# Taking a fused attention and gated MLP batch by batch instead of in pairs, with q loaded in long runs and turned by VectorE

## The chip, the cores and the metric

The kernel runs on one core of a Trainium2 chip. The metric is the device time of one execution in microseconds. Each timed kernel ran on the same chip as the kernel before; the rounds of both are compared. A kernel counts as faster or slower only from 2% on.

## The reference

Eight batches, eight heads, 576 tokens, 64 channels a head; all in float32, but the three MLP weights come as float64. Cut to what matters:

```python
kv  = einsum('bhsd,bhse->bhde', k, v)
out = einsum('bhsd,bhde->bhse', q, kv)           # no softmax: a 64x64 matrix per head
x   = out / sqrt(mean(out*out, -1) + 1e-6) * g_norm   # then [batch, token, head*channel]
gate_pre = sum of 5 taps of a causal convolution along the tokens, per channel
result   = (sigmoid(gate_pre) * (x @ w_val)) @ w_out
```

## The kernel before

Batches go in pairs: 2 x 576 tokens are nine chunks of 128 tokens. Per chunk, TensorE (PE) turns q, ScalarE copies it out of PSUM, PE multiplies it with kv (`raw`; kv itself is summed by PE and copied by DVE to `kvbd`, a tile with two heads' kv on its diagonal), ScalarE squares, VectorE (DVE) sums, GpSimd takes the root, DVE scales (`x`), PE turns x and ScalarE copies it out (`xT`). Then the MLP of the pair: `gate` (one copy and four taps, then a sigmoid), `val`, `gv = val * gate`, `out`. The program lists a pair's attention beside the MLP of the pair before it. A scheduler in the builder then fixes the order of the instructions on each engine.

```python
def unit_turn_q(i, c):                       # pair i, chunk c
    pq = ps("tp", [P, HP, P], ...)
    for hp in range(HP):
        nc.tensor.transpose(pq[:, hp, :], st["q", i, c][:, 2 * hp:2 * hp + 2, :], ident[:])
    qT = work.tile([P, HP, P], FP32, tag="qT", bufs=3, ...)
    nc.scalar.copy(out=qT[:], in_=pq[:])
    ...
def unit_gate(i, jt):                        # 1152 tokens at a time
    ...
    for tap in range(K - 2, -1, -1):
        back = K - 1 - tap
        nc.vector.scalar_tensor_tensor(out=gb[:, :, back:S], in0=xb[:, :, 0:S - back], ...)
    nc.scalar.activation(out=gate[:], in_=gate[:], func=AF.Sigmoid)
def unit_out(i, c):
    po = ps("mm", [P, C], ...)               # val and out share three PSUM buffers
    ...
    ot = work.tile([P, C], FP32, tag="ot", bufs=3, ...)
    nc.scalar.copy(out=ot[:], in_=po[:])
    nc.scalar.dma_start(out=rows_out[row:row + P, :], in_=ot[:])      # ScalarE's queue
...
for i in range(NP + 1):
    before = mlp(i - 1) if i > 0 else [... conversions of the weights ...]
    merge(attention(i) if i < NP else [], before)
```

Of the kernel before, what the change touches and what calls it, by code (L numbers as in the profile page):

```python
# [9 lines left out]
FP32 = mybir.dt.float32  # L10
U32 = mybir.dt.uint32
AF = mybir.ActivationFunctionType
# [8 lines left out]
def kernel(  # L21
# [11 lines left out]
    """Batches go in pairs: 2 * 576 tokens are nine full chunks of 128, the middle one half of each.  # L33

    The attention's output is normalised in [token, channel], where a head's channels lie in a row,
    and then goes to [channel, token], in which the convolution is a sum of shifted rows and the
    two products need no further transpose.

    The three MLP weights come as float64, in raw bits: the chip rounds them to float32, the widest
    type that its engines compute in.  # L40
    """
    nc = tc.nc
    B, H, S, D = q.shape
    C = H * D                # channels
    HP = H // 2              # pairs of heads: 128 channels each
    NJ = S // P              # full chunks of a batch
    SF = NJ * P
    T = S - SF               # tokens of a batch behind them
    NK = C // P
    NP = B // 2  # L50
    S2 = 2 * S               # tokens of a pair
    NC = S2 // P             # chunks of a pair
    NV = 3                   # parts of a pair's tokens in the value product
    SV = S2 // NV
    K = moe_conv_w.shape[0]
    assert 2 * T == P and NC * P == S2 and SV <= 512 and C <= 512
# [10 lines left out]
    # k's and v's last T tokens; the rows behind them stay zero.  # L67
# [6 lines left out]
    # Both heads' kv on the diagonal, zeros beside them.  # L74
    kv_bd = []
    for i in range(4):
        t = const.tile([P, HP, P], FP32, name=f"kvbd{i}")
        nc.vector.memset(t[:], 0.0)
        kv_bd.append(t)
# [4 lines left out]

    st = {}

    def load_kv(b):
        for n, (name, src) in enumerate((("k", k), ("v", v))):
            st[name, b] = []
            for i in range(2):  # L90
                t = loads.tile([P, H // 2, NJ, D], FP32, tag=f"{name}{i}", name=f"{name}{i}_{b}")
                nc.sync.dma_start(
                    out=t[:].rearrange("p h j d -> p h (j d)"),
                    in_=src[b, i * H // 2:(i + 1) * H // 2, 0:SF, :].rearrange(
                        "h (p j) d -> p h (j d)", j=NJ),
                )
                st[name, b].append(t)
            nc.sync.dma_start(
                out=tails[b % 2][n][0:T], in_=src[b, :, SF:S, :].rearrange("h s d -> s h d"),
            )  # L100

    def batches(i, c):
        """A chunk's rows of each batch: (rows, batch, first token)."""
        lo, hi = c * P, (c + 1) * P
        found = []
        for bb in range(2):
            first, end = max(lo, bb * S), min(hi, (bb + 1) * S)
            if first < end:
                found.append((slice(first - lo, end - lo), 2 * i + bb, first - bb * S))
        return found  # L110

    def load_q(i, c):
        t = loads.tile([P, H, D], FP32, tag="q", bufs=NC, name=f"q{i}_{c}")
        for rows, b, first in batches(i, c):
            nc.sync.dma_start(
                out=t[rows],
                in_=q[b, :, first:first + rows.stop - rows.start, :].rearrange("h s d -> s h d"),
            )
        st["q", i, c] = t

    load_kv(0)
    for c in range(NC):
        load_q(0, c)
        if c == 1:
            load_kv(1)
# [14 lines left out]
    def narrow(key, dst):  # L140
        """In words of a value's bits: lo has the mantissa's lower 32, hi its upper 20 below the
        exponent and the sign. Beyond float32's exponents it gives zero and infinity."""
# [5 lines left out]
        # The exponent in float32's bias, kept within 0..255, in its place, with the sign.  # L148
# [13 lines left out]
        # The mantissa times 2**20: a whole number, with lo behind its point.  # L162
# [20 lines left out]
    # The norm is a sum here, not a mean: its root of D goes to the gain.  # L183
# [14 lines left out]
    def unit_kv(b, hp):  # L198
# [4 lines left out]
        for j in range(NJ + 1):  # L203
            for r in range(2):
                half, h = divmod(2 * hp + r, H // 2)
                nc.tensor.matmul(  # L206
                    kvp[r * D:(r + 1) * D, hp, :],
                    st["k", b][half][:, h, j, :] if j < NJ else kl[:, 2 * hp + r, :],
                    st["v", b][half][:, h, j, :] if j < NJ else vl[:, 2 * hp + r, :],
                    start=(j == 0), stop=(j == NJ),  # L210
                )
        if hp == HP - 1:
            for r in range(2):
                rows = slice(r * D, (r + 1) * D)
                nc.vector.tensor_copy(kv_bd[b % 4][rows, :, rows], kvp[rows])
            if b + 2 < B:
                load_kv(b + 2)

    def unit_turn_q(i, c):
        pq = ps("tp", [P, HP, P], f"qTps{i}_{c}")  # L220
        for hp in range(HP):
            nc.tensor.transpose(pq[:, hp, :], st["q", i, c][:, 2 * hp:2 * hp + 2, :], ident[:])  # L222
        qT = work.tile([P, HP, P], FP32, tag="qT", bufs=3, name=f"qT{i}_{c}")
        nc.scalar.copy(out=qT[:], in_=pq[:])  # L224
        st["qT", i, c] = qT
        if i + 1 < NP:
            load_q(i + 1, c)

    def unit_norm(i, c):
        qT = st["qT", i, c]  # L230
        raw = ps("raw", [P, C], f"raw{i}_{c}")
        for hp in range(HP):
            for rows, b, _ in batches(i, c):
                nc.tensor.matmul(  # L234
                    raw[rows, hp * P:(hp + 1) * P], qT[:, hp, rows],
                    kv_bd[b % 4][:, hp, :],
                    start=True, stop=True,
                )
        sq = work.tile([P, C], FP32, tag="sq", name=f"sq{i}_{c}")
        nc.scalar.activation(out=sq[:], in_=raw[:], func=AF.Square)  # L240
        ss = work.tile([P, H], FP32, tag="ss", bufs=3, name=f"ss{i}_{c}")
        nc.vector.reduce_sum(  # L242
            out=ss[:], in_=sq[:].rearrange("p (h e) -> p h e", h=H), axis=AX.X,
        )
        nc.gpsimd.tensor_scalar(  # L245
            out=ss[:], in0=ss[:], scalar1=D * EPS, scalar2=None, op0=ALU.add,
        )
        rt = work.tile([P, H], FP32, tag="rt", bufs=3, name=f"rt{i}_{c}")
        nc.gpsimd.tensor_tensor(out=rt[:], in0=ss[:], in1=mhalf[:], op=ALU.pow)  # L249
        x = work.tile([P, C], FP32, tag="x", bufs=4, name=f"x{i}_{c}")  # L250
        nc.vector.tensor_tensor(  # L251
            out=x[:].rearrange("p (h e) -> p h e", h=H),
            in0=raw[:].rearrange("p (h e) -> p h e", h=H),
            in1=rt[:].unsqueeze(2).broadcast_to((P, H, D)),
            op=ALU.mult,
        )
        st["x", i, c] = x

    def unit_turn_x(i, c):
        if c == 0:  # L260
            st["xT", i] = work.tile([P, NK, S2], FP32, tag="xT", name=f"xT{i}")
        px = ps("tp", [P, NK, P], f"xTps{i}_{c}")
        for kc in range(NK):
            nc.tensor.transpose(px[:, kc, :], st["x", i, c][:, kc * P:(kc + 1) * P], ident[:])  # L264
        nc.scalar.activation(  # L265
            out=st["xT", i][:, :, c * P:(c + 1) * P], in_=px[:], func=AF.Copy, scale=gcol[:],
        )

    def unit_gate(i, jt):
        x = st["xT", i][:, jt, :]  # L270
        gate = work.tile([P, S2], FP32, tag="gate", bufs=3, name=f"gate{i}_{jt}")
        nc.scalar.activation(out=gate[:], in_=x, func=AF.Copy, scale=cwT[:, jt, K - 1:K])  # L272
        xb = x.rearrange("p (b s) -> p b s", b=2)
        gb = gate[:].rearrange("p (b s) -> p b s", b=2)
        for tap in range(K - 2, -1, -1):
            back = K - 1 - tap
            nc.vector.scalar_tensor_tensor(  # L277
                out=gb[:, :, back:S], in0=xb[:, :, 0:S - back], scalar=cwT[:, jt, tap:tap + 1],
                in1=gb[:, :, back:S], op0=ALU.mult, op1=ALU.add,
            )  # L280
        nc.scalar.activation(out=gate[:], in_=gate[:], func=AF.Sigmoid)  # L281
        st["gate", i, jt] = gate

    def unit_val(i, jt):
        gv = work.tile([P, S2], FP32, tag=f"gv{jt}", bufs=1, name=f"gv{i}_{jt}")
        for n in range(NV):
            cols = slice(n * SV, (n + 1) * SV)
            val = ps("mm", [P, SV], f"val{i}_{jt}_{n}")
            for kc in range(NK):
                nc.tensor.matmul(  # L290
                    val[:], wval[:, kc, jt * P:(jt + 1) * P], st["xT", i][:, kc, cols],
                    start=(kc == 0), stop=(kc == NK - 1),
                )
            nc.vector.tensor_tensor(  # L294
                out=gv[:, cols], in0=val[:], in1=st["gate", i, jt][:, cols], op=ALU.mult,
# [90 lines left out]
```

## Time and profile before

| | before |
|---|---|
| median, rounds of the changed kernel | 407.05 us (406.83 to 407.52, 4 runs) |
| span of the profiled run | 406.9 us |
| PE busy | 358.3 us, 88% |
| first val to the next pair's first val | 86.6 us for two batches, 43.3 a batch |

A pair in the middle of the trace, from val to val (the columns are the stretch, its length and the busy time of PE, its weight loads, DVE, ScalarE and GpSimd, with the number of records; then granted clock, DMA share and GB/s; a record is one instruction of the trace, and a float32 product shows as two: val's 192 products are the 384 records of L290 on its page):

```profile
160.00:246.57 86.57, 85.33 (x485) 52.41 (x481) 41.01 (x50) 29.58 (x45) 19.32 (x18) 1.00 0.43 110
```

The waits of PE in the trace before, besides those for the first loads (columns: who waited, for whom, us in total, times, longest):

```profile
PE val L290 <- DVE gv L294: 12.9, 4, 5.6
PE raw L234 <- DVE x L251: 9.4, 2, 6.7
PE xTps L264 <- DVE x L251: 3.9, 2, 2.1
```

Eight waits that matter, all but two of them (1.0 us each) at the start and at the last pair. The row of TensorE's granted clock in 40 slices (9 is full):

```profile
PEclk9989698769999999999999999999999999799999
```

Behind the start it is full, but for one slice near the end, behind PE's wait for the last pair's gates.

### The profile page before, as it was taken

Reading aid. Unit: us, or ns where it says so; the run is one execution under the profiler, and the core shown is the slowest. Engines: PE = TensorE matmul, PEld = TensorE weight load, DVE = VectorE, ACT = ScalarE, POOL = GpSimd, SP = SyncE. Lnnn points to the kernel's source line nnn. Section 1 sums busy time; section 2 is a strip of 40 time slices with the busy share of each in tenths; the row PEclk is TensorE's granted clock in tenths of the full one; section 3 lists DMA queues with packets and bytes.
Section 4 is the critical chain, followed back from the end, with each engine's and each line's share of the span. In section 5 each row is a group of like instructions: output and inputs, shape, how many; then the busy total and the mean of one; then the engine's idle time right before and its main releaser. Section 6 shows DMA issues by size and latency. Waiting matters only on the chain.

```text
span 406.9 us, 4827 instructions
## 1 busy us (share of the span) xinstructions
PE 358.3 (88%) x1924; PEld 221.1 (54%) x1924; DVE 197.3 (48%) x274; ACT 122.1 (30%) x178; POOL 82.1 (20%) x87
## 2 busy tenths in 40 slices
PE   0665776769999999999999999899999994999996
PEld 0554654536665555656655555666655552555442
DVE  6368666987432212995431126986222129951000
ACT  1023432443122335333133334422223352120111
POOL 2042644002323211005131130024232110000000
PEclk9989698769999999999999999999999999799999
DMA  7999999491272231293713310000011210000222
GB/s 231 301 275 252 288 278 187 129 208 52 66 170 77 79 103 53 84 239 117 156 52 103 93 64 26 2 2 0 2 52 52 76 54 0 0 2 1 77 77 77
DMA packets 69398, 42.28 MB, mean 104 GB/s; under 512 B 47355, under 2 KB 63739, under 8 KB 69376
## 3 DMA queue, kind: packets, MB, share of 16 engines
q1 hardware_dynamic: 62848, 28.32, 30.5%
q10 hardware_dynamic: 5344, 9.44, 6.6%
q0 software_dynamic: 1184, 4.22, 3.1%
q8 instruction: 15, 0.25, 0.3%
q14 instruction: 7, 0.06, 0.1%
HBM read 32.53 MB, written 9.44 MB: 103 GB/s over the span
## 4 chain that ended last, share of the span: by engine, by line
PE 78%; DVE 10%; POOL 3%; ACT 3%; DMA 3%; issue 1%; SPq 1%; POOLq 0%; ACTq 0%
PE out L304 31%; PE val L290 29%; PE raw L234 8%; DVE gate L277 5%; PE kv L206 4%; PE xTps L264 3%; DMA vl<-in_v_dram 3%; PE qTps L222 3%; POOL rt L249 2%; DVE ss L242 1%; DVE x L251 1%; ACT gate L281 1%; POOL ss L245 1%; ACT gate L272 1%; DVE gv L294 1%
## 5 line engine op out<-in xcount | busy, mean ns | idle before, releaser
L290 PE MATMUL val<-xT,wval 128*128 128x384 f32 x384 | 134.7, 507 | 13.0 <-DVE gv L294 12.9
L304 PE MATMUL out<-wout,gv 128*128 128x512 f32 x288 | 128.5, 593 | 0.0
L290 PEld LDWEIGHTS val<-xT,wval 128*128 128x128 f32 x384 | 74.2, 198 | 63.6 <-DVE gv L294 14.2
L277 DVE SCALAR_TENSOR_TENSOR gate<-xT,cwT,gate 128x1148 f32<-128x1148 f32 (+3 forms) x64 | 86.8, 1407 | 18.4 <-ACT gate L272 18.2
L304 PEld LDWEIGHTS out<-wout,gv 128*128 128x128 f32 x288 | 52.6, 190 | 56.3 <-issue 56.0
L249 POOL TENSOR_TENSOR rt<-ss,mhalf 128x8 f32<-128x8 f32 x36 | 60.1, 1668 | 3.0
L245 POOL TENSOR_SCALAR ss<-ss 128x8 f32<-128x8 f32 x36 | 16.2, 449 | 215.0 <-DVE ss L242 214.8
L251 DVE TENSOR_TENSOR x<-raw,rt 128x512 f32<-128x512 f32 x36 | 24.9, 692 | 70.6 <-POOL rt L249 62.9
L309 ACT COPY ot<-out 128x512 f32<-128x512 f32 x36 | 21.1, 586 | 110.0 <-PE out L304 110.0
L242 DVE TENSOR_REDUCE ss<-sq 128x8 f32<-128x512 f32 x36 | 24.6, 682 | 53.5 <-ACT sq L240 53.5
L234 PE MATMUL raw<-kvbd,qT 128*128 128x128 f32 (+1 forms) x320 | 41.5, 289 | 9.4 <-DVE x L251 9.4
L234 PEld LDWEIGHTS raw<-kvbd,qT 128*128 128x128 f32 (+1 forms) x320 | 36.8, 185 | 17.5 <-issue 12.1
L240 ACT ACTIVATE sq<-raw 128x512 f32<-128x512 f32 x36 | 21.5, 598 | 56.3 <-PE raw L234 56.2
L206 PE MATMUL kv<-v,k 128*64 128x64 f32 x512 | 25.7, 250 | 14.3 <-DMA v<-in_v_dram 14.3
L224 ACT COPY qT<-qTps 128x512 f32<-128x512 f32 x36 | 20.8, 587 | 51.9 <-PE qTps L222 51.7
L294 DVE TENSOR_TENSOR gv<-val,gate 128x384 f32<-128x384 f32 x48 | 25.4, 553 | 22.4 <-PE val L290 20.4
L206 PEld LDWEIGHTS kv<-v,k 128*64 128x64 f32 x512 | 21.9, 160 | 22.3 <-issue 21.9
L281 ACT ACTIVATE gate<-gate 128x1152 f32<-128x1152 f32 x16 | 18.6, 1167 | 50.3 <-DVE gate L277 50.3
L265 ACT ACTIVATE xT<-xTps,gcol 128x512 f32<-128x512 f32 x36 | 24.4, 689 | 8.1 <-PE xTps L264 8.1
L264 PE MATMUL xTps<-ident,x 128*128 128x128 f32 x144 | 22.1, 282 | 3.9 <-DVE x L251 3.9
L264 PEld LDWEIGHTS xTps<-ident,x 128*128 128x128 f32 x144 | 17.7, 145 | 12.8 <-issue 12.8
L222 PE MATMUL qTps<-ident,q 128*128 128x128 f32 x144 | 22.8, 292 | 0.7 <-ACT qT L224 0.7
(45 smaller groups left out, 111.6 us busy)
## 6 DMA issues: line engine op xcount, KB each, us to landing
out_dram<-ot ACTq DMA_DIRECT2D x36, 256.0 KB, 2.0
k<-in_k_dram SPq DMA_DIRECT2D x16, 512.0 KB, 5.1
v<-in_v_dram SPq DMA_DIRECT2D x16, 512.0 KB, 7.8
q<-in_q_dram SPq DMA_DIRECT2D x32, 256.0 KB, 6.5
w_wval<-in_moe_w_val_dram POOLq DMA_DIRECT2D x4, 512.0 KB, 7.6
w_wout<-in_moe_w_out_dram POOLq DMA_DIRECT2D x4, 512.0 KB, 7.0
kl<-in_k_dram SPq DMA_DIRECT2D x8, 128.0 KB, 5.8
vl<-in_v_dram SPq DMA_DIRECT2D x8, 128.0 KB, 8.3
```

The lines of the kernel that those rows point to most:

```text
L206: nc.tensor.matmul(kvp[r * D:(r + 1) * D, hp, :], st["k", b][half][:, h, j, :] if j < NJ else kl[:, 2 * hp + r, :], st["v", b][half][:, h, ...
L222: nc.tensor.transpose(pq[:, hp, :], st["q", i, c][:, 2 * hp:2 * hp + 2, :], ident[:])
L234: nc.tensor.matmul(raw[rows, hp * P:(hp + 1) * P], qT[:, hp, rows], kv_bd[b % 4][:, hp, :], start=True, stop=True,)
L242: nc.vector.reduce_sum(out=ss[:], in_=sq[:].rearrange("p (h e) -> p h e", h=H), axis=AX.X,)
L249: nc.gpsimd.tensor_tensor(out=rt[:], in0=ss[:], in1=mhalf[:], op=ALU.pow)
L251: nc.vector.tensor_tensor(out=x[:].rearrange("p (h e) -> p h e", h=H), in0=raw[:].rearrange("p (h e) -> p h e", h=H), in1=rt[:].unsqueeze( ...
L264: nc.tensor.transpose(px[:, kc, :], st["x", i, c][:, kc * P:(kc + 1) * P], ident[:])
L265: nc.scalar.activation(out=st["xT", i][:, :, c * P:(c + 1) * P], in_=px[:], func=AF.Copy, scale=gcol[:],)
L277: nc.vector.scalar_tensor_tensor(out=gb[:, :, back:S], in0=xb[:, :, 0:S - back], scalar=cwT[:, jt, tap:tap + 1], in1=gb[:, :, back:S], op0 ...
L290: nc.tensor.matmul(val[:], wval[:, kc, jt * P:(jt + 1) * P], st["xT", i][:, kc, cols], start=(kc == 0), stop=(kc == NK - 1),)
L294: nc.vector.tensor_tensor(out=gv[:, cols], in0=val[:], in1=st["gate", i, jt][:, cols], op=ALU.mult,)
L304: nc.tensor.matmul(po[:], st["gv", i, jt][:, c * P:(c + 1) * P], wout[:, jt, :], start=(jt == 0), stop=(jt == NK - 1),)
```

## The change

Its intent: no transposes of q on PE and no copies of them on ScalarE, and q's transfers in runs of some 4 kB instead of 256 B. For that q is loaded twice, so that a DVE transpose in 32 x 32 blocks puts it into [channel, token]. The blocks give the token order (n, t), in which token t*18+n stands at n*32+t; a shift of the convolution by one token is then a shift by 32 columns, with four halo rows before each batch in x. Batches go one by one. An output chunk holds four values of n, so it goes out in four transfers, and these are put on the queue of the loads. Batch 1's k and v are loaded last, behind the q of batches 0 and 1. The core of the diff:

```diff
+    def load_q(b, hp):
+        ...
+        for half in range(2):
+            for r in range(2):
+                nc.sync.dma_start(out=flat[first:first + TB, 0:run],
+                    in_=q[b, 2 * hp + r].rearrange("(t n) d -> t (n d)", t=TB)[...])
...
-    def unit_turn_q(i, c):
-        pq = ps("tp", [P, HP, P], f"qTps{i}_{c}")
-        for hp in range(HP):
-            nc.tensor.transpose(pq[:, hp, :], st["q", i, c][:, 2 * hp:2 * hp + 2, :], ident[:])
-        qT = work.tile([P, HP, P], FP32, tag="qT", bufs=3, name=f"qT{i}_{c}")
-        nc.scalar.copy(out=qT[:], in_=pq[:])
+    def unit_turn_q(b, hp):
+        ...
+        nc.vector.transpose(out=st["qT", b][:, hp, :], in_=st["q", b, hp][:, :, 0:TB])
...
+            for kc in range(NK):             # halo rows, on GpSimd
+                row = xT[:, kc, :].rearrange("p (n t) -> p n t", t=TB)
+                nc.gpsimd.tensor_copy(row[:, 0:K - 1, 1:TB], row[:, NB:NB + K - 1, 0:TB - 1])
...
-        gate = work.tile([P, S2], FP32, tag="gate", bufs=3, name=f"gate{i}_{jt}")
+        gate = work.tile([P, S], FP32, tag="gate", bufs=4, name=f"gate{b}_{jt}")
...
-        nc.scalar.dma_start(out=rows_out[row:row + P, :], in_=ot[:])
+        for j in range(HB):
+            bb, n = divmod(c * HB + j, NB)
+            nc.sync.dma_start(
+                out=rows_out[2 * i + bb, n], in_=ot[j * TB:(j + 1) * TB, :])
...
-    for i in range(NP + 1):
+    for b in range(B + 1):
```

## The prediction

Some passages of the prediction are cut, each cut marked. Terms of its sums go with them, those for DVE's turn of q. With these terms in, DVE's work came to about 240 us, the conversions, turns and kvbd of the start to 29 us, and the first gv to 7 us behind its stage's first val; what is still printed adds up to less. The forecast's last sum has all its terms in print, 120 + 293 + 39 = 452, said as 450; in the 120 and the 293 the turns are counted. That an engine keeps to its listed order was taken as given; in this case e13 and e14 show it, further down (their records follow the given lists one for one).

> **What bounds the kernel now.** I read the page's shares first, then the chain of work that ended last, then the order of time on TensorE (PE) in the middle, because a share over the whole span mixes a slow start with a dense middle.
>
> ```profile
> PE 358.3 (88%) x1924; PEld 221.1 (54%) x1924; DVE 197.3 (48%) x274; ACT 122.1 (30%) x178; POOL 82.1 (20%) x87
> PE   0665776769999999999999999899999994999996
> DMA  7999999491272231293713310000011210000222
> ```
>
> The PE is the busiest, and nearly full from about 90 us to 330 us; the DMA engines are full only in the first 60 us. The chain of work of one pair of batches:
>
> ```profile
> 160.07 7.94 PE val L290 x24
> 171.60 1.07 ACT gate L281
> 173.31 2.20 PE val L290 x6
> 196.33 7.74 PE val L290 x24
> 228.63 3.44 PE out L304 x8
> 246.64 7.94 PE val L290 x24
> ```
>
> From one pair's first val (160.07) to the next one's (246.64) are 86.6 us, and only about 1.0 us of it is a wait of the PE (for gv, before 173.31). So the middle is bound by matmuls: a val record takes 7.74/24 = 0.32 us, an out record 3.44/8 = 0.43 us. Ends of the run, where PE does wait:
>
> ```profile
> 72.28 9.37 DVE gate L277 x7
> 84.82 2.93 PE val L290 x4
> 334.57 8.11 DVE gate L277 x7
> 345.83 26.45 PE val L290 x72
> 372.28 30.91 PE out L304 x72
> ```
>
> Both gates at the start and the end are waits of the PE for VectorE (DVE): gate 0 can be used only when its four taps, interleaved with gate 1's, are through.
>
> [...] after 5.25 us of idle, the 4 records at 84.82 took 2.93 us, 0.73 each instead of 0.32. [...] The page of the kernel before counts 47355 of 69398 packets under 512 B, and slices of 231 to 301 GB/s while the engines are full.
>
> **The change, part by part.** The groups concerned:
>
> ```profile
> L222 PE MATMUL qTps<-ident,q 128*128 128x128 f32 x144 | 22.8, 292 | 0.7 <-ACT qT L224 0.7
> L224 ACT COPY qT<-qTps 128x512 f32<-128x512 f32 x36 | 20.8, 587 | 51.9 <-PE qTps L222 51.7
> L249 POOL TENSOR_TENSOR rt<-ss,mhalf 128x8 f32<-128x8 f32 x36 | 60.1, 1668 | 3.0
> ```
>
> Removed on PE: 144 transposes of q. Their slot in the stream is 0.11 us (starts of neighbouring groups of four lie 0.43 us apart), so 144 x 0.11 = 15.7 us, not the 22.8 us busy, which overlap. Added on PE: the half chunk of 64 tokens is now alone in each batch. Two halves side by side took 1.02 us per pair of batches; alone I expect 8 x 0.11 = 0.88 us per batch, so 8 x 0.88 - 4 x 1.02 = +2.9 us. val in 288 columns instead of 384 has the same columns: 0.242 us a record. Net on PE: -13 us, about 319 us of matmul slots in all, 39.9 per batch.
>
> Removed on ScalarE: 36 copies, 20.8 us, beside other work. Added on DVE: [...]64 more gate instructions (twice as many, half as long: spacing [...]0.67 us against 10.68/8 = 1.34 now), 16 more gv, 4 more ss and x: about 240 us, still under PE. Transfers: q grows from 9.4 to 8x16x32x4480 B = 18.4 MB, in runs of 4480 B instead of 256 B; output becomes 144 transfers on the queue of the loads instead of 36 on ScalarE's. 51 MB at over 250 GB/s is some 200 us, so bytes don't bind.
>
> If PE stayed as dense as now, that would give about 407 - 13 = 394. But the built program's order says it won't. I went through it engine by engine with the trace's durations: raw 0.9, sq 0.6, ss 0.68, POOL's two steps 0.24 to 0.6 + 1.67, x 0.69: about 5.2 us from raw to x, and POOL gives a chunk per 2.0 us.
>
> *Start.* The first turns of q stand in the DVE's order between the conversions of the weights, the fourth behind nearly all eight. A conversion is 7 instructions, 4 x 0.34 + 3 x 0.6 = 3.15 us. They begin when cwT is there (14.4 us, as now); 8 x 3.15 + [...]kvbd 0.9 = 29, and some 2 us of waiting for weights (three buffers, 7 us to land) end at about 45. Only then can the first batch's raw be finished. Five chunks through two raw buffers, with x before the next ss in the DVE's order, take until about 66, against a first gv at 84 now. But then only half as much has been done: in the kernel before, two batches' attention.
>
> *Batch 0's MLP and batch 1's attention.* kv of batch 1 is behind out 2 in PE's order, because its loads are issued last. So: 3 vals 5.8, wait for the gate (8 gate instructions, a table load of 1.28) 2, other vals 10, out 13.8, kv 2.6, to about 100. Then batch 1's raw-to-x chains run with next to nothing beside them, 20 us with 8 us of work in it: val of batch 1 starts at about 120, val of batch 2 at 165 (now: the same point, 2 batches' val done, at 160).
>
> *The later stages.* Three waits of PE per batch:
> - At the gate. The first gv is ready 0.7 (copy) + 5.4 (8 taps)[...] + 0.5 = 7 us after the stage's first val. Now it is 12.6 us, but a pair offers 3 x 2.58 us of val, kv and turns for it. Here val and gv share three PSUM buffers with out, and in ScalarE's order the copies of the last out chunks stand behind the gates and the next batch's squares. So two or one buffers are left: in the order, val 1 of batches 1, 3, 5 waits for the first gv after 2 vals (3.9 us), and of batches 2, 4, 6 after one single val (1.9 us). That is 3 to 5 us of wait.
> - With one buffer, each val waits for the gv of the one before (0.5 us each), and the second gv stands behind six gate instructions (4 us): 4 to 5 us more in those batches.
> - Behind out: the fourth turn of q stands behind kvbd, so raw of the first two chunks is finished in the out stage, and PE waits for x of both (1.5 + 1 us); in batches 3 and 5 also for kvbd and for an out buffer (3.5 us).
>
> Stages 1 to 6 from val to val, by hand: 45, 50, 51, 50, 51, 46 us, sum 293, with PE work of 40 to 42 in each. Last batch: 17 of val with a 1.5 us wait, out 5 x 3.44 = 17.2, copy, four issues and the landing 4: 39. Sum: 120 + 293 + 39 = 452. The half clock[...] may add 1 us a stage; my steps may be too pessimistic by as much. I say 450.
>
> **Rivals.** *PE stays full* (394, or 385 with a quicker start): for it speaks the middle of the kernel before, which has the same scheduler and waits just 1 us per pair; against it, the order, which in before offers PE 12 us of other work at that point and here 2 to 4. *A better tail and start decide* (about 400): now the PE waits about 12 us before the last pair's val (333.28 to 345.83), and out of one batch instead of two is uncovered; that is worth some 10 us, and in my sum already. *Transfers become the bound* (above 460): output, q and k, v share one queue in order, and a load behind an output waits for ScalarE's late copy; I found the loads still 10 us early by the sizes and 250 GB/s. *DVE as the bound*: 240 us of 450, no; it binds by its order, not by its sum.
>
> **Range and chances.** The middle's stages are six repetitions of the same kind of step, so an error of 3 us in one counts 18 us; the start is good to some 6 us. 8 in 10: 428 to 470. Faster would need the stalls to be under a fourth of what I find: 5%. Within 2% (399 to 415): 5%. Slower: 90%.
>
> **What would show it.** PE's busy time falls to about 340 to 350 with a share under 80%; idle before val, for gv, 25 to 40 us in all instead of 13; idle before raw, for x, over 15 us instead of 9; first val at about 66, the second batch's at 120[...]. Wrong I would be if the waits of PE for gv stay near 13 us, if the clock row stays full and stages are 42 us long, or if loads of q or k, v end PE's waits.

## The result, and the profile after

The changed kernel takes **481.93 us** (480.97 to 482.86, 4 runs) against 407.05. The ratio is 1.1836, with a 95% interval of 1.1814 to 1.1857. Ratios here are the mean time of one kernel's fast runs over the mean of the other's fast runs of the same rounds, so not quite the ratio of the medians that are quoted.

The page of the changed kernel:

```profile
PE 374.6 (78%) x1924; PEld 242.0 (50%) x1924; DVE 235.0 (49%) x392; ACT 111.8 (23%) x182; POOL 90.0 (19%) x139
PE   0412659984798969988897959979797977899895
PEclk9999979999799988999897898999799798999998
DMA  7997951064004930049502960019800820112012
L234 DVE STREAM_TRANSPOSE qT<-q 128x576 f32<-128x576 f32 x32 | 24.6, 770 | 0.1
```

PE has as many records as before, is busy 16 us longer and yet never stays at 9 for long. Its clock row now has a 7 or 8 in every second or third slice. The transfers come in bursts with pauses, so they are not what bounds the kernel, and a turn of q takes 770 ns. The waits of PE:

```profile
PE raw L244 <- DVE qT L234: 40.4, 9, 7.3
PE raw L244 <- DVE x L260: 17.1, 14, 3.6
PE xTps L273 <- DVE x L260: 9.6, 4, 3.0
PE val L301 <- DVE gv L307: 9.1, 7, 3.7
```

The largest wait is new: `raw` for the turned q. The DVE hardly waited before its turns (0.1 us in the group above), so q was there; the turn stood behind other work in DVE's own order. The stages from one batch's first val to the next (first val at 67.19, then as in the left column; columns as above):

```profile
122.78:169.19 46.41, 42.77 (x183) 27.00 (x183) 23.75 (x37) 13.27 (x23) 10.45 (x14) 0.98 0.43 108
169.19:222.62 53.43, 47.07 (x296) 30.42 (x294) 25.51 (x41) 13.63 (x24) 10.46 (x14) 0.94 0.29 75
222.62:280.26 57.64, 50.88 (x248) 32.55 (x248) 26.31 (x41) 13.39 (x23) 10.52 (x14) 0.88 0.55 133
...
sum 316.86, PE 274.87 PEld 175.15 DVE 150.38 ACT 81.57 POOL 62.93; mean PE 45.81 PEld 29.19 DVE 25.06 ACT 13.60 POOL 10.49
```

The six middle stages take 317 us. PE is idle for 42 of them. It is busy 45.8 us a stage, and in the third stage the granted clock is 0.88. Where that comes from is seen in the timeline of PE there (start, us, what, and in brackets the wait before it):

```profile
251.67 1.02 PE L317 MATMUL out<-wout,gv 128*128 128x512 f32 x2
...
256.95 0.85 PE L244 MATMUL raw<-kvbd,qT 128*64 128x128 f32 x4 [1.77 <-DVE qT L234]
259.01 2.08 PE L317 MATMUL out<-wout,gv 128*128 128x512 f32 x2 [1.22 <-ACT ot L322]
```

The two out records at 259.01 take 2.08 us, those at 251.67 took 1.02: half clock, after two waits of 1.77 and 1.22 us (the granted clock is 0.50 from 258.2 to 268.4). Added up over windows of 1 us, the half clock covers 56 us behind the 69th microsecond, against 20 us in the kernel before. The second wait is for `ot`, the copy of an earlier output chunk on ScalarE:

```profile
257.42 1.07 ACT L249 ACTIVATE sq<-raw 64x512 f32<-64x512 f32 x2 [16.18 <-PE raw L244]
258.39 1.06 ACT L322 COPY ot<-out 128x512 f32<-128x512 f32 x2
```

ScalarE stood for 16.18 us at a square of the next batch, because its order has that square ahead of two copies of outputs. This is what "stands in the order" means: PE had both chunks done by 252.69 us, and their copies, listed behind the square, began at 258.39.

### The profile page after: what moved, and what is told of

It reads as the page before. It is cut to its first block, busy times and chain, and to the rows that moved or that the text cites. A ratio compares the mean times of both kernels' runs of the same rounds, so it can differ in the third digit from the quotient of the medians.

```text
span 479.6 us, 5304 instructions
## 1 busy us (share of the span) xinstructions
PE 374.6 (78%) x1924; PEld 242.0 (50%) x1924; DVE 235.0 (49%) x392; ACT 111.8 (23%) x182; POOL 90.0 (19%) x139
## 4 chain that ended last, share of the span: by engine, by line
PE 56%; DVE 17%; POOL 7%; DMA 7%; issue 6%; ACT 4%; SPq 1%; DVEq 0%; POOLq 0%
PE val L301 22%; PE out L317 21%; DVE gate L290 9%; PE raw L244 8%; POOL rt L258 6%; PE xTps L273 3%; PE kv L218 3%; DMA w_wval<-in_moe_w_val_dram 2%; DVE ss L251 2%; DMA w_wout<-in_moe_w_out_dram 2%; DVE qT L234 2%; DVE x L260 2%; DMA w_cw<-in_moe_conv_w_dram 1%; DMA v<-in_v_dram 1%; ACT gate L287 1%
## 5 line engine op out<-in xcount | busy, mean ns | idle before, releaser
L301 PE MATMUL val<-xT,wval 128*128 128x288 f32 x512 | 145.4, 439 | 12.7 <-DVE gv L307 9.1
L301 PEld LDWEIGHTS val<-xT,wval 128*128 128x128 f32 x512 | 101.7, 205 | 44.8 <-DVE gv L307 11.9
L290 DVE SCALAR_TENSOR_TENSOR gate<-xT,cwT,gate 128x576 f32<-128x576 f32 x128 | 97.2, 809 | 35.0 <-ACT gate L287 34.8
L244 PE MATMUL raw<-kvbd,qT 128*128 128x128 f32 (+1 forms) x320 | 62.2, 330 | 60.8 <-DVE qT L234 40.4
L258 POOL TENSOR_TENSOR rt<-ss,mhalf 128x8 f32<-128x8 f32 (+1 forms) x40 | 66.7, 1666 | 3.0
L260 DVE TENSOR_TENSOR x<-raw,rt 128x512 f32<-128x512 f32 (+1 forms) x40 | 27.6, 689 | 69.7 <-POOL rt L258 67.6
L307 DVE TENSOR_TENSOR gv<-val,gate 128x288 f32<-128x288 f32 x64 | 28.5, 452 | 51.8 <-PE val L301 50.0
L251 DVE TENSOR_REDUCE ss<-sq 128x8 f32<-128x512 f32 (+1 forms) x40 | 26.7, 678 | 21.4 <-ACT sq L249 21.3
L276 ACT ACTIVATE xT<-xTps,gcol 128x512 f32<-128x512 f32 (+1 forms) x40 | 25.4, 642 | 39.5 <-PE xTps L273 39.3
L273 PE MATMUL xTps<-ident,x 128*128 128x128 f32 (+1 forms) x160 | 24.8, 285 | 9.6 <-DVE x L260 9.6
L322 ACT COPY ot<-out 128x512 f32<-128x512 f32 x36 | 20.6, 584 | 39.4 <-PE out L317 28.2
L234 DVE STREAM_TRANSPOSE qT<-q 128x576 f32<-128x576 f32 x32 | 24.6, 770 | 0.1
```

What stands on the lines that cost most here:

```text
L234: nc.vector.transpose(out=st["qT", b][:, hp, :], in_=st["q", b, hp][:, :, 0:TB])
L244: nc.tensor.matmul(raw[0:m, hp * P:(hp + 1) * P], st["qT", b][:, hp, cols], kv_bd[b % 2][:, hp, :], start=True, stop=True,)
L251: nc.vector.reduce_sum(out=ss[0:m], in_=sq[0:m].rearrange("p (h e) -> p h e", h=H), axis=AX.X,)
L258: nc.gpsimd.tensor_tensor(out=rt[0:m], in0=ss[0:m], in1=mhalf[0:m], op=ALU.pow)
L260: nc.vector.tensor_tensor(out=x[0:m].rearrange("p (h e) -> p h e", h=H), in0=raw[0:m].rearrange("p (h e) -> p h e", h=H), in1=rt[0:m].unsq ...
L273: nc.tensor.transpose(px[:, kc, 0:m], st["x", b, c][0:m, kc * P:(kc + 1) * P], ident[0:m, 0:m])
```

## The experiments

All outputs are right. Every kernel was timed in 3 rounds (e16 in 5), with 4 runs each in the tables; the kernel before had medians of 407.3 to 407.6 us in them. Of these runs one was slow, a run of e7, and it is left out below.

### Which part of the change costs

**e1_warm: fill one wait per batch.** Seven idle matmuls behind the first val of each batch but the first, in the unused part of that val's PSUM bank.

```diff
+            if b > 0 and jt == 0 and n == 0:
+                for _ in range(WARM):
+                    nc.tensor.matmul(
+                        val[:, SV:C], wval[:, 0, 0:P], xTs[b % 3][:, NK - 1, HALO:HALO + C - SV],
+                        start=True, stop=True,
```

> The changed kernel with 7 idle matmuls (14 records of 224 columns, about 2.6 us) put on TensorE right behind the first val of batches 1 to 7, just where it then stands still for the gate. They write a part of the PSUM bank that nothing reads. Theory 'half clock': the waits end when they ended before, but the half-clock stretches after them (176-183, 231-234, 285-292, 340-347, 398-402 us in the changed kernel's trace, 27 us in all) go, and as half of such a stretch is lost, the time falls by 9 to 14 us, to 468 to 473. Rival 'the clock only mirrors idle time': no gain, 480 to 484. Rival 'TensorE had no time to spare there': 7 x 2.6 = 18 us more, 500.

Measured: 482.90 us, 1.1854 (1.1813 to 1.1896). A miss. PE's waits did shrink (for the turned q from 40.4 to 30.1 us, for gv from 9.1 to 4.3), but behind the 69th microsecond PE was busy 15 us longer, and the time stayed. Of the half clock only part went: 42 of 56 us are left, some of it at new places in the out stages (207 to 210 and 316 to 320 us).

**e2_single: smaller batches alone.** Batches one by one, but q turned by PE as before, tokens in their natural order, one output transfer per chunk on ScalarE's queue, and batch 1's k and v loaded early.

```diff
-    for i in range(NP + 1):
+    for b in range(B + 1):
...
+        m = P if c < NJ else T
+        t = loads.tile([P, H, D], FP32, tag="q", bufs=9, name=f"q{b}_{c}")
+        nc.sync.dma_start(
+            out=t[0:m], in_=q[b, :, c * P:c * P + m, :].rearrange("h s d -> s h d"))
```

> Batches one by one, but q as in the kernel before: 256-byte runs, turned by TensorE and copied by ScalarE, tokens in their natural order, one output transfer per chunk on ScalarE's queue, batch 1's k and v loaded early. This is the granularity alone. Theory 'granularity': with half the val per gate, TensorE waits as in the changed kernel, 445 to 470. Theory 'q's turn on VectorE and the order it forces': q's transposes and kv fill the wait at the gate (2 to 3 vals 4 to 6 us, kv 2.6, two chunks of transposes 0.9, against 7 us), so about 415 to 430, of which 10 are the single half chunks and 17.6 - 15.7 = 2 more transposes. I lean to the second, 425.

Measured: **401.18 us**, 0.9843 (0.9822 to 0.9864), so 6 us less than before; under 2%, and below the ranges of both theories. Its page shows a PE that is hardly ever idle:

```profile
PE 362.0 (91%) x2084; PEld 247.2 (62%) x2084; DVE 211.1 (53%) x360; ACT 132.1 (33%) x222; POOL 84.3 (21%) x95
PE   1547757999999999999999999999999999997996
```

Halved batches, to which the prediction put the waits, do not by themselves make them.

**e3_turn: the other half of the change.** Pairs of batches as before, with DVE's turns, the order (n, t) and the outputs on the loads' queue. It is a large edit; its core is `unit_turn_q` and `load_q` of the change with `for i in range(NP + 1)` kept.

> Pairs of batches as in the kernel before, but q in long runs, turned by VectorE, tokens in (n,t) order with halo rows, 144 output transfers on the loads' queue. This is the other half of the change alone (three q buffers instead of four and single buffers for the conversion of the weights, for room). Theory 'granularity': dense, 395 to 410. Theory 'q's turn': the turns stand between gates and kvbd in VectorE's order, raw waits for them, one wait of 3 to 6 us a pair and half clock after it, 420 to 445. I lean to 420.

Measured: 485.08 us, 1.1894 (1.1862 to 1.1927). A miss, above the ranges of both theories. PE waits 56.0 us for the turns. So the loss comes without one-by-one batches.

**e4_kv1: batch 1's k and v right behind batch 0's q.**

```diff
         load_q(0, hp)
+    load_kv(1)
```

> The changed kernel with batch 1's k and v loaded right behind batch 0's q instead of last. In the changed kernel TensorE has little beside batch 1's attention from 100 to 123 us. Theory: batch 1's kv, raw and turns then lie beside batch 0's val and out, so the stage from the first val to the second batch's (55.6 us) shrinks to about 46 to 48 us and the time falls by 7 to 10 us, to 472 to 475. Rival: the same waits for gates and buffers take its place, or the start gets later by the 1.2 MB (5 us): 478 to 483.

Measured: 489.37 us, 1.2003 (1.1976 to 1.203). A miss, and 7 us slower than the changed kernel: the earlier load makes nothing faster here.

**e5_peturn: q turned by PE again.** The changed kernel, but q comes in runs of 256 B in the order (n, t) and is turned by PE; outputs stay on the loads' queue. (With it batch 1's k and v come early again, as in e2 and e4.)

```diff
-        nc.vector.transpose(out=st["qT", b][:, hp, :], in_=st["q", b, hp][:, :, 0:TB])
+        for hp in range(HP):
+            nc.tensor.transpose(
+                pq[:, hp, 0:m], st["q", b, c][0:m, 2 * hp:2 * hp + 2, :], ident[0:m, 0:m])
+        nc.scalar.copy(out=qT[:, :, 0:m], in_=pq[:, :, 0:m])
```

> Everything of the change except VectorE's turn: batches one by one, tokens in (n,t) order with halo rows, 144 output transfers on the loads' queue, but q in 256-byte runs once, turned by TensorE chunk by chunk (batch 1's k and v early, as in the run with batches one by one). Theory A, formed from the second and third experiment (401 and 485 us): the loss lies in VectorE's turn, so this is 398 to 412. Rival B: the halo copies (last chunk first), the token order or the outputs on the loads' queue carry it, 440 to 485.

Measured: 468.73 us, 1.1515 (1.1463 to 1.1567). A miss of theory A by some 60 us, and inside the rival's range. There is no turn on DVE left to wait for, and yet most of the loss is there: PE now waits 27.7 us for gv. The wait for the turned q is where the loss shows, not what makes it.

**e6_ahead: turns one batch ahead.**

```diff
+            if n < HP and b + 1 < B:
+                units.append((0.1, lambda hp=n: unit_turn_q(b + 1, hp)))
```

> The changed kernel with VectorE turning the q of the next batch but one stage earlier: the turns of batch b+1 are given out among batch b's attention, so that a batch's raw waits for no turn made in its own stage; nothing else is changed. Theory A: what costs is not the turns' 24.6 us on VectorE but where they stand (behind gates and kvbd, so that a batch's five chains from raw to x only begin in the out stage). Then the middle's stages fall from 54 to 43 to 46 us and the time to 410 to 435 (the start, 67 us, stays). Rival: VectorE's work or the halved gate as such binds, 465 to 485.

Measured: 471.55 us, 1.1553 (1.1501 to 1.1605). A miss: 10 us of the 75. The wait for the turn falls to 19.7 us (all of it in the start), and waits for x and kvbd take its place.

**e7_actq: only the queue of the outputs.**

```diff
-            nc.sync.dma_start(
+            nc.scalar.dma_start(
                 out=rows_out[2 * i + bb, n], in_=ot[j * TB:(j + 1) * TB, :])
```

> The changed kernel with its 144 output transfers issued on ScalarE's queue, as in the kernel before, so that no load stands behind an output that waits for its copy. Rival 'one queue' (SyncE waits 218 us for these copies): a load comes earlier and the time falls by 10 us or more. My theory: no wait of VectorE for q is in the trace and one of TensorE for v at most, so no gain, 478 to 490, rather slower, as 144 issues then stand in ScalarE's order.

Measured: **431.58 us**, the median of the three fast runs (429.38 to 435.33), 1.0608 (1.0519 to 1.0697). A fourth run took 437.51 and counts as slow; with it the median is 433.46, which is where the 48 us in e9's expectation comes from. A miss, and the most useful one: one word takes 50 of the 75 us away.

```profile
PE 357.2 (83%) x1924; PEld 236.9 (55%) x1924; DVE 232.4 (54%) x392; ACT 113.9 (26%) x182; POOL 91.3 (21%) x139
...
PE raw L244 <- DVE qT L234: 19.6, 3, 7.4
```

The first line is of its page, the second of its waits: what is left of the wait for the turn are three waits in the start.

### Is it the transfers or the order?

Two explanations were open for what the queue costs here: its transfers stand behind each other, or the builder's scheduler makes another order out of it. The built programs do differ. Written down from ScalarE's list for one batch (g a gate's copy, S a sigmoid, q a square of the next batch's raw, x a copy of xT, o an output copy with its chunk's number):

```
changed kernel: g g g g S S S S q4 q3 [o7] q2 x [o8] q1 x [o0] q0 [o1] x x [o2] x
e7_actq:        g g g g S S S q4 S q3 q2 x [o0] q1 x [o1] q0 [o2] x x [o3] x
```

In the changed kernel's trace one or two output copies of each of batches 0 to 5 (here 7 and 8) stand behind the next batch's gates and its first squares (three of a pair's nine); in e7's none does. The middle is where it tells: the six stages take 264.4 us in e7 and 316.9 in the changed kernel.

**e8_best** (turns ahead, conversions of the output weights behind the first x's, batch 1's k and v early; loads' queue) and **e9_ot7** (seven `ot` buffers instead of three, so that PE need not wait for late copies):

```diff
+            with tc.issue_after(ins.ins):        # e8_best, beside the edits of e4 and e6
+                unit_weights(2 * NK - c)
...
-        ot = work.tile([P, C], FP32, tag="ot", bufs=3, name=f"ot{i}_{c}")
+        ot = work.tile([P, C], FP32, tag="ot", bufs=7, name=f"ot{i}_{c}")     # e9_ot7
```

> Turns one batch ahead as in the run before, and besides the conversions of the output weights put behind the x of the first batch's chunks in VectorE's order (before, all eight stood ahead of the fourth turn of the first q), and batch 1's k and v loaded early. Theory A: the first val comes at 50 to 55 us instead of 67 and batch 1's attention lies beside batch 0's MLP, so 12 to 20 us less than the run with the turns ahead alone, 390 to 415. Rival: the conversions only move into the gate stage of batch 0, same time as that run.

> The changed kernel with 7 buffers instead of 3 for the copied outputs, the queue left as it is. In the built order of the changed kernel up to four of the nine copies of a pair's outputs stand one batch later in ScalarE's order, behind the next gates, sigmoids and the first two squares, and hold one or two of the three PSUM buffers that val needs. With 7 buffers most copies are back in their own stage. Theory 'late copies hold val's PSUM buffers' (which I now hold for the 48 us that the output queue was worth): 430 to 450. Rival 'loads stand behind outputs in the one queue': the queue is unchanged, so 475 to 485.

Measured: e8_best 482.67 us, 1.1853 (1.1797 to 1.1909); e9_ot7 492.31 us, 1.2081 (1.2044 to 1.2118). Both missed. With seven buffers the wait for gv falls to 1.3 us, but the outs of a batch then run more in one go (in one batch 28 of 32 records, 12.18 us), and the chains from raw to x stand alone behind them: xTps waits 31.7 us and raw 27.1 us for x. No copy stands behind the next batch's gates any more, so such copies alone are not the cause; what is left is the order as a whole. One mark goes with every slow order, though: the time from a chunk's last out record to its copy. It is over 3 us for 16 of 36 chunks in the changed kernel (46.0 at the longest), and for 6 to 25 in e3, e5, e6, e8, e9 and, further down, e14; in e7, e10, e11, e12 and e15 it is never over 1.4 us, and in e13 once over 3.

**e10_single_sync: e2_single with its 36 outputs on the loads' queue.**

```diff
-        nc.scalar.dma_start(out=rows_out[row:row + P, :], in_=ot[:])
+        nc.sync.dma_start(out=rows_out[row:row + P, :], in_=ot[:])
```

> The kernel with batches one by one and q as before (401 us), its 36 output transfers of 256 KB moved to the loads' queue, nothing else. In the built order every copy stays in its own stage. Theory 'late copies': the queue as such costs nothing, 399 to 406. Rival 'one queue for loads and outputs': 430 or more.

Measured: 404.54 us, 0.9925 (0.989 to 0.996). The queue as such costs 3 us where its outputs are 36.

**e11_peturn_actq** is e5_peturn and **e12_best_actq** is e8_best with the outputs on ScalarE's queue, by the edit of e7:

```diff
-            nc.sync.dma_start(
+            nc.scalar.dma_start(
```

> Token order, halo rows and four output transfers a chunk as in the changed kernel, q turned by TensorE, outputs on ScalarE's queue: the fifth experiment (469 us) with only the queue undone. Theory: the middle's stages come to 43 to 46 us, the start stays 6 us later than with the natural order, 408 to 420. Rival 'the token order and the halo copies cost by themselves': 440 or more.

> Turns one batch ahead, conversions of the output weights behind the first batch's x, batch 1's k and v early (together 483 us on the loads' queue), now with the outputs on ScalarE's queue. Theory: with copies in their own stage the turns ahead let raw start early, stages of 42 to 44 us, 108 to the second val, 40 at the end: 398 to 412. Rival: VectorE's turn holds raw up all the same, as in the run with ScalarE's queue alone, 428 to 438.

Measured: e11_peturn_actq 415.16 us, 1.0188 (1.0145 to 1.0231), 54 less than e5; e12_best_actq 420.67 us, 1.0327 (1.0287 to 1.0368), 62 less than e8. e11 is inside its theory's range, e12 between the ranges of its two. With the queue undone, the mending of the start does help (432 to 421).

**e13_order and e14_actq_order: order and transfers crossed.** e13 has the changed kernel's transfers and queue, but PE, DVE, ScalarE and GpSimd are held to the order that e7 was built with. e14 has e7's queue, and the engines are held to the changed kernel's order. The edges order the issue and add no wait (with such edges for its own order, in e17 below, the changed kernel takes 481.88 us for 481.93).

```diff
+    traced = list(nc.cur_bb.bb.instructions)
+    for runs in ORDER.values():
+        ...
+                    tc.add_manual_dep(
+                        traced[k], traced[last].name,
+                        mybir.DependencyInfo(
+                            mybir.DependencyClass.NoSync, mybir.DependencyReason.DATA),
+                        reason="order",
+                    )
```

> The changed kernel with its outputs left on the loads' queue, but TensorE, VectorE, ScalarE and GpSimd held, instruction by instruction, to the order that the build chose for the run with the outputs on ScalarE's queue (433 us). The order is given as edges of issue without waits; instructions, buffers and transfers are the changed kernel's. Theory 'order': 428 to 442. Rival 'the transfers on the one queue': 470 to 485.

> The reverse: outputs on ScalarE's queue, the four engines held to the order of the changed kernel. Theory 'order': 472 to 492. Rival 'the transfers on the one queue': 428 to 442.

Measured: e13_order **437.05 us**, 1.0745 (1.0704 to 1.0785); e14_actq_order **487.64 us**, 1.1978 (1.1958 to 1.1998). Both are inside the ranges of the theory 'order'. The traces confirm that the orders were kept: on PE, DVE, ScalarE and GpSimd e13's records follow e7's one for one (1924, 392, 182 and 139), and e14's the changed kernel's. The order costs 45 us with the loads' queue (481.93 against 437.05) and 56 with ScalarE's (487.64 against 431.58); the queues differ by 5 to 6 us, the loads' being the slower with e7's order and the faster with the changed kernel's. So the time goes with the order and not with the queue. On which of the four engines the order matters was not tried. The waits of e14 are those of the changed kernel nearly one for one, though its outputs leave by the other queue:

```profile
PE raw L317 <- DVE qT L307: 42.7, 9, 7.2
PE raw L317 <- DVE x L333: 17.0, 13, 3.6
```

**e15_turn_actq: e3_turn with the outputs on ScalarE's queue** (the same edit of one word).

> Pairs of batches with q turned by VectorE (485 us in the third experiment), outputs on ScalarE's queue. Theory 'order': most of the loss goes, 410 to 435, the pair's longer gate (10.7 us of taps for two gates) being waited for. Rival 'VectorE's turn costs in pairs whatever the queue': above 450.

Measured: 450.19 us, 1.1059 (1.1038 to 1.1081), 35 less than e3, but above the theory's range and at the edge of the rival's. In pairs, DVE's turn costs more (PE waits 32.1 us for it) than one by one (19.6 us in e7).

**e16_single_wout: the fastest that I found.** e2_single with the conversions of the output weights moved behind batch 0's first three pairs of gv.

```diff
+        if b == 0 and jt < 3:
+            with tc.issue_after(ins.ins):
+                for n in range(NK + 1 + jt, NK + 2 + jt + jt // 2):
+                    unit_weights(n)
```

> A try at a faster kernel: batches one by one with q as before (401 us), the conversions of the output weights put behind batch 0's first three pairs of gv in VectorE's order, instead of between the first batch's x. The first val's second half comes at about 46 instead of 56 us, but VectorE's sum before the first out stays: 393 to 400. Rival: out of batch 0 waits for the conversions as long as was gained, 400 to 403.

Measured: 399.76 us, 0.9815 (0.98 to 0.983) in 5 rounds: 1.85% less than the kernel before, so under the 2% as well, and 17% less than the changed one.

### What the half clock costs

**e17_held and e18_fill.** The term of the prediction that stood out by now was the half clock, the time in which PE's granted clock is 0.50. e17 is the changed kernel held to its own order (a control for the means used, with all kv sums in one PSUM bank). e18 adds 156 idle matmuls in the unused half of that bank, put into 18 waits of PE.

```diff
+    def fill(b):
+        for _ in range(FILL.get(b, 0)):
+            nc.tensor.matmul(
+                kvs[:, HP:HP + P // D, :], wval[:, 0, 0:P], wval[:, 0, 0:P],
+                start=True, stop=True,
```

> Control for the next run: the changed kernel, held instruction by instruction to its own order on PE, DVE, ScalarE and GpSimd by issue-order edges without waits, with the sums kv in one PSUM bank for all batches instead of a fresh buffer each. Every theory expects the changed kernel's time: 480 to 485 us, a ratio of 1.18 to 1.19, and half-clock stretches of some 56 us after 69 us.

> The control with 156 idle matmuls of 128 columns (0.215 us each, 33 us in all) put into the 18 waits of PE of 0.9 us or more behind the first val, each wait filled to about 85 per cent, in the unused half of kv's bank. Theory that the half clock is itself what the prediction mis-sized: PE is kept busy, the half clock goes, and with it the roughly 22 us of busy time that it costs: 458 to 466 us, a ratio of 1.125 to 1.145. Rival, that the time at half clock only stands where another engine's chain would have made PE wait anyway: 477 to 485 us with the waits longer by what the clock gives, a ratio of 1.17 to 1.19, although the half-clock stretches are gone.

Measured: e17_held 481.88 us, 1.1831 (1.18 to 1.1862), as it should be. e18_fill 487.48 us, 1.1978 (1.1946 to 1.201): slower, outside the first theory's range and 2 us above the rival's. The half clock fell from 57 to 24 us behind the 69th microsecond, so the means worked; but the stages answer differently:

| stage, from first val to first val | changed, us | e18_fill, us |
|---|---|---|
| batch 0 | 55.6 | 61.4 |
| 1 | 46.4 | 46.4 |
| 2 | 53.4 | 58.3 |
| 3 | 57.6 | 53.4 |
| 4 | 53.3 | 54.7 |
| 5 | 57.4 | 55.1 |
| 6 | 48.7 | 48.7 |
| 7, to the end | 40.0 | 40.0 |

Two stages are spoilt by the test itself: writing into kv's bank, the idle matmuls had to wait for the copies of kv (5.40 us in batch 0's stage, 5.93 in batch 2's), and only then ran. In the other stages it is nearly clean (0.96 us of such a wait in each of batches 3 and 5). In the stages of batches 3 and 5 PE is the bound for most of the time (in e18 it is busy 49.8 of 53.4 us and 51.4 of 55.1), and taking the half clock away gives 4.2 and 2.3 us: the last val ends 1.7 and 2.9 us earlier, and behind it batch 3 gains 2.5 us more and batch 5 loses 0.5 (a stretch at half clock came up at 382 to 385 us). In the stages of batches 1 and 6 it gives nothing. In the stage of batch 4 it lay from the wait at the gate to the second gv (285.5 to 292.3 us), and there it gives nothing either. The timeline of e18 in that stage (line 203 is the idle matmuls) shows why:

```profile
289.37 4.63 PE L203 MATMUL kvs<-wval 128*128 128x128 f32 x40
294.78 0.43 PE L330 MATMUL raw<-kvbd,qT 128*64 128x128 f32 x2 [0.78 <-DVE qT L320]
295.14 2.21 PE L387 MATMUL val<-xT,wval 128*128 128x288 f32 x8
...
299.86 3.90 PE L387 MATMUL val<-xT,wval 128*128 128x288 f32 x8 [2.29 <-DVE gv L393]
```

The second val now runs at full clock (2.21 us; in the changed kernel 4.18), and then PE waits 2.29 us for gv, where the changed kernel waited 0.33. DVE's gates set that end, at either clock. The third val then took 3.90 us: with that wait the half clock came back (0.50 from 299.9 to 303.3 us), which is why this stage is 1.4 us longer. The half clock of the five stages 1 and 3 to 6 cost 17.2 us of busy time in the changed kernel and 3.3 in e18; 5.1 us of that came back.

### The sum of the 75 us

| step | median, us | step's cost |
|---|---|---|
| before | 407 | |
| batches one by one, q as before (e2) | 401 | -6 |
| token order, halo rows, four output transfers per chunk and q's loads to match (e11) | 415 | +14 |
| q in long runs, turned by DVE; batch 1's k and v last (e7) | 432 | +16 |
| outputs on the loads' queue, by the built order (after) | 482 | +50 |

The steps are differences of medians, in this order; taken in pairs of batches (e15 to e3) the last one was 35. With the queue put first they look different: +3 for the queue (e2 to e10), +64 for token order, halo rows and four transfers (e5), +13 for the rest. So the 50 us belong to the queue together with what e11 brings in (the four transfers per chunk among it), and not to the queue alone. The +14 of e11 was not taken apart further.

## Why the prediction was right or wrong

The direction was right, and the size was wrong: 450 was said with 428 to 470, and 482 came.

**Right: the method.** PE would not stay full, because "the built program's order says it won't". e13 and e14 show that the order of the instructions on the engines is worth some 50 us of the time: 432 to 437 us for one order and 482 to 488 for the other, whatever the queue.

**Right: start and end.** The first val was put at 66 and came at 67.19; the second batch's at 120, and came at 122.78; the last batch at 39 us, and took 40.0. In each stage the first gv was put at 7 us, and was done at 7.7 to 7.8. A turn of q takes 0.77 us. But the busy time of PE was to fall to 340 to 350; it rose to 374.6, and that points to the fault.

**Wrong: the middle stages.** By hand they were 45, 50, 51, 50, 51 and 46 us, sum 293; they took 46.4, 53.4, 57.6, 53.3, 57.4 and 48.7, sum 316.9. By the prediction's own terms there is "PE work of 40 to 42 in each", so 240 to 252 us of work and 41 to 53 of waits:

| six middle stages | predicted, us | measured, us |
|---|---|---|
| PE idle | 41 to 53 | 42.0 |
| PE's work at full clock | 240 to 252 | 254.7 |
| half clock on top | 0 (6, set off against pessimism) | 20.2 |
| sum | 293 | 316.9 |

The third row is PE's busy time in windows of 1 us times one less the granted clock, summed up; the second is the busy time of 274.9 less that. Work and waits together were told right within 4 us (296.7 for 293), so the steps were not too pessimistic, and there was nothing to set the half clock off against. (The work is 42.4 us a stage, in the middle of before it was 42.7 a batch: of the 13 us that PE was to save, little is seen there.) The step that failed is the sentence **"The half clock [...] may add 1 us a stage; my steps may be too pessimistic by as much."** It measured 3.4 us a stage, 6 in the two worst. The step, an estimate, was set down for long single waits; but in this trace the half clock came also behind shorter ones that add up (1.77 and 1.22 us, with 0.50 from 258.2 to 268.4).

Two cautions belong to it. The half clock is that large a part of the busy time, but it is not a cost that could be had back whole. The five stages in which e18 was nearly clean (1 and 3 to 6) were put at 243 us and took 263.4. e18 removes 13.9 of their 17.2 us of half clock, and they still take 258.3. In batches 4 and 6 DVE's gates set the pace of the vals at either clock: before the third val PE waits for gv 0.33 and 0.79 us in the changed kernel, and 2.29 us both times in e18, where the second val ran at full clock. So the term is mis-sized in the account, but most of the miss does not go away with it; what else these stages would need, no run isolates.

And that the sum of the waits came out right is in part luck, because their kinds were wrong. For gv 25 to 40 us were forecast and 9.1 measured (7.2 in the six stages), under the 13 that the prediction itself named as a sign of being wrong. In their place stand 20.6 us in which `raw` waits for the turned q, a wait of PE that the prediction did not list for these stages. Some 17 of them, in batches 3 to 6, stand where the wait at the gate was expected: in PE's order the next batch's raw comes right behind the first vals, and in DVE's order its turn comes right behind the first eight gate instructions.

**Wrong in cause: the halved batches.** Against the first rival it was held that the order "in before offers PE 12 us of other work at that point and here 2 to 4", and the waits were laid to that. e2 has the halved batches, with q turned by PE, and takes 6 us less than before; e3 has whole pairs and takes 485. The order was read rightly as a list, but it had another origin.

**Wrong in cause: the queue.** "output becomes 144 transfers on the queue of the loads" was weighed as bytes and rows in a queue, and found harmless. As transfers it is indeed nearly so (e13 lies 5 us above e7, e10 3 us above e2). But the same choice changed the builder's order, worth some 50 us, and the prediction even named its trace: "in ScalarE's order the copies of the last out chunks stand behind the gates and the next batch's squares". It did not ask what had put them there. What in the builder makes 144 strided transfers on the loads' queue lead to that order, no run shows; it stays open.

**Right in part: the rivals against.** "Transfers become the bound" and "DVE as the bound" are both out: DVE is busy 235.0 us, put at 240, the DMA row is full of pauses, and no turn of q waited for a load. That the time lies in the range of "Transfers become the bound" (above 460) is chance. In the rival "A better tail and start decide" a reading was off: before 345.83 PE waited 5.6 us and not about 12, since from 333.28 on it still ran val records until 340.2. The last batch came out right all the same.

## What to carry to other kernels

When a change alters queues, buffers or granularity, compare the built order of every engine before and after, and undo the parts one at a time: the part that looked like mere transport was worth 50 of 75 us here, and the wait that headed the list was only where it showed. Price PE's half clock by stretches in which PE is mostly idle, not by the longest wait alone (here PE was busy 1.23 us from 254.8 to 258.2, and the clock was 0.50 from there to 268.4); and before filling such waits, see which engine ends the stretch: in e18 the time came back where PE did (4.2 and 2.3 us in the stages of batches 3 and 5) and not where DVE's gates did (batches 4 and 6). The pieces without the long runs and the (n, t) order, batches one by one with outputs on ScalarE's queue, are the better kernel at 399.8 us.

## The half clock in the trace after

In this one trace, behind the 60th microsecond, the granted clock is 1.00 or 0.50, and the stretches at 0.50 that end before the kernel does last 3.41, 6.83 or 10.24 us; those at 1.00 between them last 17.07 to 75.09 us, all multiples of 3.41. Cut at the ends of the stretches and every 3.41 us between, the time up to 476.7 us gives 122 windows, 105 of them at 1.00:

- In ten of the 105, PE was busy 1.39 us or less, and 0.50 followed each time (the last time at 476.7 us, where the program runs out); in the other 95 it was busy 1.59 us or more, and 0.50 never followed. A single long wait was not needed: in 254.8 to 258.2 us PE was busy 1.23 us, with waits of 1.77 and 1.22 us around one record group, and the clock was 0.50 from 258.2 to 268.4.
- Of the 17 windows at 0.50, 1.00 followed nine of the ten in which PE was busy 3.05 us or more, and none of the seven with 2.72 us or less. The tenth is 261.6 to 265.0, busy throughout, and the next 3.4 us were still at 0.50, as the two lines below show (columns as above). What made it differ, no run shows.

```profile
261.60:265.00 3.40, 3.40 (x16) 3.06 (x17) 1.38 (x2) 1.07 (x2) 1.26 (x1) 0.50 0.79 229
265.00:268.40 3.40, 3.40 (x12) 2.57 (x12) 1.28 (x2) 1.76 (x3) 2.41 (x4) 0.50 0.94 253
```

This is a count of one trace; that the bounds are the same in another is not shown.
